# The last channel output in three column pieces, stored from two DMA queues

## The chip, the cores and the metric

One core of one Trainium2 chip (TensorE, VectorE, ScalarE, GpSimd and SyncE, written PE, DVE, ACT, POOL and SP in the profile). The metric is the device time of one execution in microseconds; the kernel before takes 380.88 us (median of 6 runs). A time contains a little under 2 us outside the profile's span: the profiled run of the kernel before took 380.45 us and its span is 378.7 us.

## The reference, cut to what matters

```python
# q, k, v: (8, 12, 448, 64);  x: (8, 448, 768)
scores = scale * (q @ k.transpose(0, 1, 3, 2)) - np.log(S)
x  = merge_heads(sigmoid(scores) @ v)
h  = np.maximum(x.transpose(0, 2, 1) @ w_tok1, 0.0) @ w_tok2   # token mixing
u  = x + h.transpose(0, 2, 1)
h2 = np.maximum(u @ w_ch1, 0.0) @ w_ch2                        # channel mixing
return u + h2                                                  # (8, 448, 768), float32
```

Only the last line matters here: how the last rows of `u + h2` come out of TensorE, through VectorE's addition, to the output in HBM.

## The kernel before: the parts that matter

The kernel is written as operations with dependences and assumed durations. A planner simulates them in Python and so fixes the order in which each engine gets its instructions. The durations are only the planner's assumptions.

A batch has 448 rows, that is 3 blocks of 128 rows and a rest of 64. The rests of two batches share a fourth block: 64 partitions each. So the very last piece of work is `blk == 3` of the last batch: 128 rows (64 of batch 6, 64 of batch 7) by 768 columns.

```python
def channel2(b):
    side = b % 2
    for blk in range(4 if side else 3):
        tiles = (b - 1, b) if blk == 3 else (b,)
        for half in range(2):
            c = slice(DH * half, DH * half + DH)          # DH = 384 columns
            ps = bank(f"c2_{b}_{blk}_{half}", [128, DH])
            def ch2(ps=ps, c=c, blk=blk):
                for cb in range(NCB):                     # NCB = 12
                    w = w_ch2[cb // 4][:, cb % 4, c]
                    if blk < 3:
                        ...                               # one matmul of 128 rows
                    else:
                        for s in range(2):                # two matmuls of 64 rows, side by side
                            nc.tensor.matmul(out=ps[64 * s : 64 * s + 64, :],
                                             lhsT=h2aT[b - 1 + s][:, cb, 384:448], rhs=w, ...)
            ...
            def add(...):                                 # DVE: u = u + psum
                nc.vector.tensor_tensor(out=t, in0=t, in1=ps[:, :], op=ADD)
            a = op(f"y_{b}_{blk}_{half}", "DVE", 0.56, add, ...)
        def store(blk=blk, mine=mine):                    # after both halves are added
            for s in range(2):
                r = slice(64 * s, 64 * s + 64)
                if blk == 3:
                    nc.sync.dma_start(
                        out=out[b - 1 + s].rearrange("(p j) d -> p j d", j=J)[:, 3, :],
                        in_=mine[r, :])
                else:
                    ...                                   # the two row halves go to different rows j
        op(f"st_{b}_{blk}", "SP", 1.3, store, sum_ops[(b, blk)], [mine], rank=2)
```

## Time and profile before

The head of the page of the kernel before: the span, each engine's busy time (with its share of the span and its number of instructions), and the chain of work that ended last, by engine.

```profile
span 378.7 us, 7932 instructions
...
PE 370.8 (98%) x3243; PEld 191.3 (51%) x3243; DVE 160.6 (42%) x296; ACT 205.7 (54%) x252; POOL 118.5 (31%) x265
...
PE 90%; POOL 4%; DMA 2%; ACT 1%; DVE 1%; issue 0%; POOLq 0%
```

TensorE bounds the kernel from start to nearly the end. The change can't touch this. It touches what comes after TensorE's last matmul. The timeline of the kernel before, for this stretch (start in us, duration in us, engine, line, operation, output and inputs, count; in brackets the engine's idle time before and what ended it):

```profile
369.86 4.09 PE L925 MATMUL c<-w_ch,h2aT 128*64 128x384 f16 x48
...
372.11 0.55 DVE L940 TENSOR_TENSOR ut<-ut,c 128x384 f32<-128x384 f32 x1 [1.59 <-PE c L925]
373.99 0.55 DVE L940 TENSOR_TENSOR ut<-ut,c 128x384 f32<-128x384 f32 x1 [1.33 <-PE c L925]
374.57 1.10 SPq L950 DMA_DIRECT2D out_dram<-ut  x2
```

The line of SPq shows only that SP hands two stores to the DMA engines (0.47 and 0.59 us). The Trainium skill ("Perfetto Trace Analysis", section on the HWDGE instruction) warns that the movement of the data lies outside of this window, and here it does: the first packet moves at 375.69 and the last ends at 377.42, while both issues are over by 375.68. So the tail has to be put together from several records. From the start of the last block:

| step in the kernel before | us | cumulated |
|---|---|---|
| first matmul of the last block to the start of its last matmul | 3.77 | 3.77 |
| to the start of the last add | 0.37 | 4.13 |
| last add, 128x384 | 0.55 | 4.69 |
| to the first of the two store issues | 0.03 | 4.72 |
| first issue to the end of the last packet | 2.85 | 7.56 |
| last packet to SP's drain (SP tests that all stores have landed) | 0.44 | 8.00 |
| closing barrier of the engines, to the end of the span | 0.83 | 8.83 |

I shall call the 8.83 us **the tail**: from the first matmul of the last block to the end of the span.

### The profile page before, as it was taken

To read this page: it belongs to the slowest core of one execution; us is meant where nothing else is said; L and a number is where in the kernel's file an instruction comes from. 1 tells how busy PE (TensorE), PEld (TensorE's weight loads), DVE (VectorE), ACT (ScalarE), POOL (GpSimd) and SP (SyncE) were. 2 spreads that over 40 slices of the span, in tenths; PEclk is the share of its full clock that TensorE was granted. 3 is DMA by queue.
4 is the path that set the end of the run, shared out by engine and by line. 5 is a ranking of instruction groups with operands and counts; after the bars stand their busy time and mean duration, and the time that the engine had idled before them with its cause. 6 is when DMAs were issued, how large, how long until landed. Compare 5 with 4: busy or idle time off the path is not lost.

```text
span 378.7 us, 7932 instructions
## 1 busy us (share of the span) xinstructions
PE 370.8 (98%) x3243; PEld 191.3 (51%) x3243; DVE 160.6 (42%) x296; ACT 205.7 (54%) x252; POOL 118.5 (31%) x265
## 2 busy tenths in 40 slices
PE   8999999999999999999999999999999999999994
PEld 4555544555445554445444555444445655555662
DVE  3444434644344323453355313643432365754221
ACT  2987884486757766787678466846664130200000
POOL 9973326344344434444344343430000000000000
PEclk9999999999999999999999999999999999999999
DMA  6999999989987999999999999991103553300353
GB/s 80 181 176 205 208 210 176 153 141 184 146 126 111 174 162 235 146 120 208 190 149 161 162 180 156 145 197 39 30 16 97 113 106 94 73 2 0 85 123 85
DMA packets 98804, 50.56 MB, mean 134 GB/s; under 512 B 72336, under 2 KB 95120, under 8 KB 98768
## 3 DMA queue, kind: packets, MB, share of 16 engines
q0 software_dynamic: 24400, 21.93, 44.2%
q1 hardware_dynamic: 74368, 28.13, 40.8%
q8 instruction: 25, 0.41, 0.4%
q14 instruction: 11, 0.09, 0.1%
HBM read 43.84 MB, written 11.01 MB: 145 GB/s over the span
## 4 chain that ended last, share of the span: by engine, by line
PE 90%; POOL 4%; DMA 2%; ACT 1%; DVE 1%; issue 0%; POOLq 0%
PE c L871 30%; PE c L916 25%; PE qk L542 10%; PE xa L579 8%; PE yn L794 5%; PE k L764 5%; PE c L925 4%; DMA k<-in_k_dram 2%; POOL k L304 1%; POOL q L304 1%; POOL v L304 1%; ACT attn L557 1%; POOL w_tok L337 1%; PE xa L693 1%; PE tk L499 0%
## 5 line engine op out<-in xcount | busy, mean ns | idle before, releaser
L557 ACT ACTIVATE attn<-qk,att_bias 128x896 f16<-128x896 f32 (+1 forms) x172 | 160.9, 987 | 78.6 <-PE qk L542 78.3
L871 PE MATMUL c<-uT,w_ch 128*128 128x448 f16 x576 | 118.0, 353 | 0.1
L916 PE MATMUL c<-w_ch,h2aT 128*128 128x384 f16 x576 | 98.5, 326 | 0.0
L896 DVE TENSOR_SCALAR h2aT<-c 128x448 f16<-128x448 f32 x96 | 59.9, 624 | 77.4 <-PE c L871 77.2
L871 PEld LDWEIGHTS <-w_ch 128*128 128x128 f16 x576 | 53.4, 98 | 56.7 <-issue 11.6
L916 PEld LDWEIGHTS <-h2aT 128*128 128x128 f16 x576 | 55.2, 98 | 40.1 <-issue 4.5
L940 DVE TENSOR_TENSOR u<-u,c 128x384 f32<-128x384 f32 x48 | 26.6, 554 | 77.4 <-PE c L916 77.4
L542 PE MATMUL qk<-qT,kT 64*64 64x448 f16 x672 | 53.1, 363 | 0.2 <-ACT uT L708 0.2
L579 PE MATMUL xa<-attn,v 64*64 64x448 f16 x672 | 36.5, 350 | 0.4 <-ACT attn L557 0.4
L728 POOL COPY mark<-attn 1x1 f16<-1x1 f16 x54 | 9.6, 178 | 80.0 <-ACT attn L557 79.9
L823 ACT ACTIVATE u<-u 128x768 f16<-128x768 f32 x21 | 17.8, 846 | 25.0 <-DVE u L815 25.0
L542 PEld LDWEIGHTS <-kT 64*64 64x64 f16 x672 | 14.5, 104 | 29.8 <-issue 26.9
L815 DVE TENSOR_TENSOR u<-x,yn 128x384 f32<-128x384 f16 x48 | 24.9, 548 | 9.1 <-PE yn L794 9.1
L475 POOL COPY kp<-k 128x384 f16<-128x384 f16 (+1 forms) x54 | 21.2, 427 | 21.0 <-DMA k<-in_k_dram 16.0
L794 PE MATMUL yn<-h,w_tok 128*128 128x384 f16 x128 | 27.4, 328 | 0.0
L579 PEld LDWEIGHTS <-v 64*64 64x64 f16 x672 | 19.6, 107 | 13.2 <-issue 1.6
L612 ACT ACTIVATE xT<-xa 128x448 f16<-128x448 f32 x43 | 21.1, 547 | 9.3 <-PE xa L579 8.1
L475 POOL COPY qp<-q 128x384 f16<-128x384 f16 (+1 forms) x54 | 21.3, 430 | 9.0 <-DMA q<-in_q_dram 8.7
L764 PE MATMUL k<-x,w_tok 128*128 128x384 f16 x112 | 20.6, 327 | 0.1
L776 DVE TENSOR_SCALAR h<-k 128x384 f16<-128x384 f32 x28 | 15.4, 556 | 11.9 <-PE k L764 10.8
L315 POOL DMA_DIRECT2D k<-in_k_dram x21 | 15.0, 716 | 7.4 <-issue 5.9
L794 PEld LDWEIGHTS <-w_tok 128*128 128x128 f16 x128 | 11.0, 98 | 12.1 <-issue 5.9
(57 smaller groups left out, 186.7 us busy)
## 6 DMA issues: line engine op xcount, KB each, us to landing
out_dram<-u SPq DMA_DIRECT2D x48, 192.0 KB, 3.0
k<-in_k_dram POOLq DMA_DIRECT2D x21, 224.0 KB, 5.2
q<-in_q_dram POOLq DMA_DIRECT2D x21, 224.0 KB, 5.5
v<-in_v_dram POOLq DMA_DIRECT2D x21, 224.0 KB, 5.4
w_ch<-in_moe_w_ch_dram POOLq DMA_DIRECT2D x6, 768.0 KB, 15.9
out_dram<-ut SPq DMA_DIRECT2D x8, 192.0 KB, 3.2
v<-in_v_dram POOLq DMA_DIRECT2D x6, 112.0 KB, 4.7
x<-xT SPq DMA_TRANSPOSE x36, 4.6
```

The costliest lines, as they stand in the source:

```text
L475: nc.gpsimd.tensor_copy(out=pm[:, to, :, :], in_=src[:, fr, :, :])
L542: nc.tensor.matmul(out=ps[64 * s : 64 * s + 64, h, 0:S], lhsT=kT[64 * h : 64 * h + 64, i, s, :], rhs=qT[64 * h : 64 * h + 64, :, s, :], st ...
L557: nc.scalar.activation(out=at[:, hs, :], in_=ps[:, hs, 0:S], func=SIGMOID, bias=bias_t[:, :], scale=att_scale,)
L579: nc.tensor.matmul(out=ps[s](slice(64 * h, 64 * h + 64)), lhsT=vf[64 * s : 64 * s + 64, h, order[i], :], rhs=attn[i][64 * s : 64 * s + 64, ...
L612: nc.scalar.activation(out=xt[:, s, c0 : c0 + S], in_=ps[s](every), func=COPYF)
L764: nc.tensor.matmul(out=ps[:, :], lhsT=w_tok1[:, w1_slot(side, blk), 128 * t : 128 * t + 128], rhs=X[b][:, x_block(side, blk), c], start=(b ...
L794: nc.tensor.matmul(out=ps[:, :], lhsT=w_tok2[:, t, s0 : s0 + 2, :], rhs=h1[b][:, t, c], start=(t == 0), stop=(t == 1),)
L815: nc.vector.tensor_tensor(out=to, in0=x, in1=y, op=ADD)
L871: nc.tensor.matmul(out=to(), lhsT=w_ch1[cb // 4][:, db, 128 * (cb % 4) : 128 * (cb % 4) + 128], rhs=uT[b][:, db, :], start=(db == 0), stop ...
L896: nc.vector.tensor_scalar(out=h2aT[b][:, cb, :], in0=to(), scalar1=0.0, scalar2=None, op0=MAX)
L916: nc.tensor.matmul(out=ps[:, :], lhsT=h2aT[b][:, cb, 128 * blk : 128 * blk + 128], rhs=w, start=(cb == 0), stop=(cb == NCB - 1),)
L940: nc.vector.tensor_tensor(out=t, in0=t, in1=ps[:, :], op=ADD)
```

## The change

The intent is to leave less work behind the last matmul. The second half of the last block is cut into two pieces of 192 columns, so that there are three pieces (384, 192, 192). Each is added and stored as soon as it is there, and the two row halves are issued from two queues (SP and the idle ACT) instead of one after the other. Cut to its core:

```diff
-            for half in range(2):
-                c = slice(DH * half, DH * half + DH)
-                ps = bank(f"c2_{b}_{blk}_{half}", [128, DH])
+            final = b == B - 1 and blk == 3
+            cuts = [(0, DH), (DH, 576), (576, D)] if final else [(0, DH), (DH, D)]
+            def store(c=slice(0, D), blk=blk, mine=mine, final=final):
+                for s in range(2):
+                    r = slice(64 * s, 64 * s + 64)
+                    queue = nc.scalar if final and s else nc.sync
+                    if blk == 3:
+                        queue.dma_start(
+                            out=out[b - 1 + s].rearrange("(p j) d -> p j d", j=J)[:, 3, c],
+                            in_=mine[r, c],
+                        )
+                    ...
+            for half, (z0, z1) in enumerate(cuts):
+                c = slice(z0, z1)
+                ps = bank(f"c2_{b}_{blk}_{half}", [128, z1 - z0])
...
-                a = op(f"y_{b}_{blk}_{half}", "DVE", 0.56, add, ...)
+                a = op(f"y_{b}_{blk}_{half}", "DVE", 0.06 + (z1 - z0) * 0.0013, add, ...)
+                if final:
+                    op(f"st_{b}_{blk}_{half}", "SP", 0.7, lambda ...: store(c), [a], [mine], rank=2)
-            op(f"st_{b}_{blk}", "SP", 1.3, store, sum_ops[(b, blk)], [mine], rank=2)
+            if not final:
+                op(f"st_{b}_{blk}", "SP", 1.3, store, sum_ops[(b, blk)], [mine], rank=2)
```

More of the change, by code (lines that the diff above doesn't have):

```diff
@@ L907, in channel2 @@
             tiles = (b - 1, b) if blk == 3 else (b,)
-            for half in range(2):
-                c = slice(DH * half, DH * half + DH)
-                ps = bank(f"c2_{b}_{blk}_{half}", [128, DH])
+            final = b == B - 1 and blk == 3
+            cuts = [(0, DH), (DH, 576), (576, D)] if final else [(0, DH), (DH, D)]
+            mine = ut[b // 2] if blk == 3 else u[b]
+            def store(c=slice(0, D), blk=blk, mine=mine, final=final):
[7 more added lines that the diff above has]
+                        )
+                    else:
+                        j = blk + 4 * (s != side)
+                        queue.dma_start(
+                            out=out[b].rearrange("(p j) d -> p j d", j=J)[:, j, :],
+                            in_=mine[r, blk, :],
+                        )
+            for half, (z0, z1) in enumerate(cuts):
+                c = slice(z0, z1)
+                ps = bank(f"c2_{b}_{blk}_{half}", [128, z1 - z0])
                 def ch2(ps=ps, c=c, blk=blk):
@@ L933, in channel2 @@
                 need = [x for t in tiles for x in ch1_ops[t]] + ch2_ld
-                o = op(f"C2_{b}_{blk}_{half}", "PE", 12 * mm(DH), ch2, need, [ps, *(h2aT[t] for t in tiles), *w_ch2])
+                o = op(f"C2_{b}_{blk}_{half}", "PE", 12 * mm(z1 - z0), ch2, need, [ps, *(h2aT[t] for t in tiles), *w_ch2])
                 ops.append(o)
-                mine = ut[b // 2] if blk == 3 else u[b]
                 def add(ps=ps, c=c, blk=blk, mine=mine):
@@ L942, in channel2 @@
                 sums = [x for t in tiles for x in u_ops[t]]
-                a = op(f"y_{b}_{blk}_{half}", "DVE", 0.56, add, [o, *sums], [ps, mine], rank=-1)
+                a = op(f"y_{b}_{blk}_{half}", "DVE", 0.06 + (z1 - z0) * 0.0013, add, [o, *sums], [ps, mine], rank=-1)
                 sum_ops.setdefault((b, blk), []).append(a)
-            def store(blk=blk, mine=mine):
-                for s in range(2):
-                    r = slice(64 * s, 64 * s + 64)
-                    if blk == 3:
-                        nc.sync.dma_start(
-                            out=out[b - 1 + s].rearrange("(p j) d -> p j d", j=J)[:, 3, :],
-                            in_=mine[r, :],
-                        )
-                    else:
-                        j = blk + 4 * (s != side)
-                        nc.sync.dma_start(
-                            out=out[b].rearrange("(p j) d -> p j d", j=J)[:, j, :],
-                            in_=mine[r, blk, :],
-                        )
-            op(f"st_{b}_{blk}", "SP", 1.3, store, sum_ops[(b, blk)], [mine], rank=2)
+                if final:
+                    op(f"st_{b}_{blk}_{half}", "SP", 0.7, lambda store=store, c=c: store(c), [a], [mine], rank=2)
+            if not final:
+                op(f"st_{b}_{blk}", "SP", 1.3, store, sum_ops[(b, blk)], [mine], rank=2)
         return ops
```

## The prediction

> **What bounds the kernel.** TensorE: the page gives PE 370.8 us busy (98%) of a 378.7 us span, and the chain that ended last is 90% PE. The change touches only the end. In the timeline the last block (48 matmuls, 64 output rows by 384 columns) starts at 369.86, its last matmul at 373.62. What follows is a tail of 5.1 us without TensorE:
>
> - last add, 128x384: 373.99 to 374.54 (0.55 us);
> - two store issues on the SP queue, one after the other: 374.57 (0.47 us), 375.09 (0.59 us);
> - packets from 375.69 to 377.41 (8 of 3072 bytes on each engine, 121 to 250 ns each);
> - SP sees the last landing at 377.79; then 0.9 us of closing barrier, to 378.69.
>
> **What changes.** The second half of the last block becomes two pieces of 192 columns; each of three pieces is added and stored alone (six issues instead of two), half of the rows from SP, half from ACT, idle since about 330 us. The bytes (384 KB) stay.
>
> 1. TensorE: a pair of matmuls starts every 162 ns at 384 columns; I estimate 82 at 192. Weight loads should not bind: the transposes, also 64-column pairs, start every 55 ns. 24 pairs of 82 instead of 12 of 162: +0.03 us.
> 2. Last add: VectorE groups 256, 384, 448 columns wide (424, 556, 624 ns) give 1.04 ns a column, so 0.35 us at 192: -0.20.
> 3. Issue: the last row half no longer queues behind the other: up to -0.5. The Trainium skill ("DMA: Bandwidth & Descriptors", section on issuing engines) says that several issuing engines save only the sequencer's issue time; "Perfetto Trace Analysis" (HWDGE instruction) has the descriptor generator locked by one at a time. No run shows yet whether the lock eats this; I count half, -0.25.
> 4. Data: after the last issue 96 KB are left (8 packets of 768 bytes an engine) instead of 384 KB; the rest goes out while TensorE and VectorE still work. 1.7 us of packets become about 0.6 to 0.9 (packets of 896 bytes, another queue, took 87 ns): -0.8, the largest term.
> 5. Receipt (0.38 us from last packet to SP) and barrier (0.9 us) stay.
>
> All of it is on the critical path: nothing else runs there. Sum: about -1.2 us; less a little for a slow first issue on ACT (5 of 56 store issues on SP took 1.4 to 1.6 us): -1.1 us.
>
> **Predicted: 379.8 us, 8 in 10 between 379.0 and 380.6. Faster by over 2%: 0.01; within 2%: 0.97; slower by over 2%: 0.02.** The trace's span should be about 377.6 instead of 378.7.
>
> **What would show each step.** Pairs of 192 columns 80 to 90 ns apart (over 110: weight-bound) (1); last add about 354 ns (2); SP's and ACT's last issues starting within 50 ns of each other, ACT's lasting near 0.5 (no lock) or near 1.0 us (lock) (3); last packet 0.7 to 1.1 us after the last piece's first, before 376.7 (4); last landing seen at 376.4 to 377.0, 0.9 us from there to the end (5).
>
> **What would make it wrong.** (a) ACT's first issues are slow and pile up. (b) The adds wait for the earlier piece's store to finish reading the shared tile: +1 to +3 us. (c) The kernel's planner gets a marginally different duration for every channel add (0.5592 instead of 0.56) and may order earlier work differently: a microsecond either way. (d) Small rows land no faster, as fixed latency governs: gain only 0.3 to 0.5 us.

## The result

| | median us | lowest to highest | runs |
|---|---|---|---|
| before | 380.88 | 380.54 to 380.92 | 6 |
| changed | 380.44 | 379.62 to 381.07 | 6 |

The ratio of the times is 0.9991, with a 95% interval of 0.9978 to 1.0003. (A ratio is the mean time of one kernel's runs over that of the other's of the same rounds, so not quite the ratio of the medians above.) So this first look shows a gain of about 0.4 us that can't be told from none. In the profile the span went from 378.7 to 378.6 us. Yet the tail is clearly shorter. The timeline of the changed kernel:

```profile
370.65 4.12 PE L945 MATMUL c<-w_ch,h2aT 128*64 128x384 f16 x72
...
372.90 0.55 DVE L959 TENSOR_TENSOR ut<-ut,c 128x384 f32<-128x384 f32 x1 [1.59 <-PE c L945]
373.48 2.18 SPq L917 DMA_DIRECT2D out_dram<-ut  x3
373.49 2.21 ACTq L917 DMA_DIRECT2D out_dram<-ut  x3
373.82 0.35 DVE L959 TENSOR_TENSOR ut<-ut,c 128x192 f32<-128x192 f32 x1 [0.37 <-PE c L945]
374.81 0.35 DVE L959 TENSOR_TENSOR ut<-ut,c 128x192 f32<-128x192 f32 x1 [0.64 <-PE c L945]
```

The first line counts all 72 matmuls of the last block under its first shape; 48 of them have 192 columns. Two things are to be seen. First, the last block begins at 370.65 instead of 369.86: the changed kernel reached its changed part 0.79 us later. Second, from there on it is faster: its tail is 7.91 us instead of 8.83.

| step | before | changed | difference |
|---|---|---|---|
| first to last matmul of the last block (starts) | 3.77 | 3.88 | +0.11 |
| to the start of the last add | 0.37 | 0.29 | -0.08 |
| last add | 0.55 | 0.36 | -0.20 |
| to the last piece's first issue | 0.03 | 0.03 | 0.00 |
| that issue to the end of the last packet | 2.85 | 1.78 | -1.07 |
| last packet to SP's drain | 0.44 | 0.74 | +0.30 |
| closing barrier | 0.83 | 0.85 | +0.02 |
| tail | 8.83 | 7.91 | -0.92 |

The view of the DMA issues for the end of both kernels (output and input, queue, operation, count, KB of each, median us from issue to landing). Before:

```profile
out_dram<-ut SPq DMA_DIRECT2D x2, 192.0 KB, 2.7
```

Changed:

```profile
out_dram<-ut SPq DMA_DIRECT2D x1, 96.0 KB, 2.1
out_dram<-ut ACTq DMA_DIRECT2D x1, 96.0 KB, 2.4
out_dram<-ut SPq DMA_DIRECT2D x2, 48.0 KB, 1.9
out_dram<-ut ACTq DMA_DIRECT2D x2, 48.0 KB, 2.1
```

A store of 48 KB needs 1.9 us on SP's queue against 2.7 for 192 KB: a quarter of the bytes takes about 70% of the time.

Three questions are left: why the block started later, where the +0.30 at the end comes from, and which half of the change (the pieces or the second queue) does the work.

### The profile page after: what moved, and what is told of

Same layout as the page of the kernel before. It is cut to its first block, busy times and chain, and to the rows that moved or that the text cites. A ratio compares the mean times of both kernels' runs of the same rounds, so it can differ in the third digit from the quotient of the medians.

```text
span 378.6 us, 7990 instructions
## 1 busy us (share of the span) xinstructions
PE 370.4 (98%) x3267; PEld 191.6 (51%) x3267; DVE 161.0 (43%) x297; ACT 205.9 (54%) x252; POOL 118.4 (31%) x265
## 4 chain that ended last, share of the span: by engine, by line
PE 90%; DMA 3%; POOL 3%; ACT 1%; DVE 1%; issue 0%; POOLq 0%
PE c L871 30%; PE c L936 25%; PE qk L542 10%; PE xa L579 8%; PE yn L794 5%; PE k L764 5%; PE c L945 4%; DMA k<-in_k_dram 3%; ACT attn L557 1%; POOL k L304 1%; POOL q L304 1%; POOL w_tok L337 1%; PE xa L693 1%; PE tk L499 0%; PE xb L632 0%
```

## The experiments

Twelve kernels ran. All gave a correct result. All of them list the same instructions in the same order on every engine up to the last block, apart from the stores named below; this was compared in the built programs, and the records of PE's matmuls, DVE and ACT in the 14 traces agree with it. "Tail" is always read from the kernel's own trace. Times of whole runs scatter by a microsecond.

### The same two kernels again

No edit. Theory A: the later start of the last block is chance. Rival B: the change slows the start of the kernel.

> The kernel before, unchanged, as a control. Theory A (the change gains about 0.9 us in the tail, and the rest of the difference between the two traces is chance in the loading phase): the tail, from the start of the last block's first matmul to the end of the span, is again 8.8 us (8.83 in the first trace), the time from one build of it to another scatters by some tenths, ratio 1.000 within 0.002; the moment at which the last block starts may differ from 369.86 by up to 0.8 us. Rival B (the change slows the start of the kernel): the last block starts within 0.2 us of 369.86 again.

> The changed kernel, unchanged, as a second look. Theory A: the tail from the last block's first matmul is again 7.9 us, while the start of the last block moves from its 370.65, and the time lies about 0.9 us under the kernel before (ratio 0.9976). Rival B: the last block starts again near 370.6, and the ratio is again near 0.999.

| trace | last block starts | tail | time, median us (range) | ratio to before |
|---|---|---|---|---|
| before, first | 369.86 | 8.83 | 380.88 (380.54 to 380.92) | |
| before, again | 371.32 | 8.82 | 381.40 (380.94 to 383.50) | 1.0011 (0.9984 to 1.0038) |
| changed, first | 370.65 | 7.91 | 380.44 (379.62 to 381.07) | 0.9991 (0.9978 to 1.0003) |
| changed, again | 370.05 | 7.90 | 379.95 (379.54 to 382.03) | 0.9975 (0.9946 to 1.0004) |

The tails repeat to 0.01 us; the start of the last block moved by 1.46 us between two executions of an identical kernel, and this time the changed kernel's came earlier. So theory A holds: the 0.79 us were chance. Here is where it arises. Per stretch of time: us, then busy time (and instructions) of PE, PEld, DVE, ACT and POOL, granted clock, DMA share, GB/s. Before, first trace:

```profile
10.00:25.00 15.00, 14.19 (x188) 7.60 (x184) 6.52 (x15) 14.05 (x19) 14.57 (x22) 1.00 1.19 177
25.00:41.00 16.00, 15.02 (x217) 8.55 (x218) 9.08 (x18) 13.20 (x19) 5.91 (x11) 1.00 1.25 203
41.00:369.00 328.00, 327.83 (x2739) 167.58 (x2735) 139.91 (x251) 175.23 (x212) 88.77 (x213) 1.00 0.84 131
```

The same kernel again:

```profile
10.00:25.00 15.00, 13.68 (x186) 7.47 (x186) 6.24 (x14) 13.09 (x18) 13.29 (x21) 1.00 1.14 167
25.00:41.00 16.00, 14.82 (x192) 8.05 (x192) 8.70 (x17) 13.45 (x19) 6.42 (x10) 1.00 1.24 202
41.00:369.00 328.00, 327.67 (x2751) 167.56 (x2752) 140.14 (x251) 176.34 (x213) 89.47 (x215) 1.00 0.83 131
```

While the first inputs are being loaded, the DMA brought 177 GB/s in one execution and 167 in the other, and PE worked less. The lag changes mostly at PE's transposes of q and k, which need the inputs that are being loaded; the largest single step (from 0.4 to 1.2 us) is at this group, which waited in the second execution and not in the first. First trace, then the second:

```profile
17.34 0.58 PE L499 MATMUL tk<-ident,k 128*64 128x128 f16 x14
18.58 0.58 PE L499 MATMUL tk<-ident,k 128*64 128x128 f16 x14 [0.84 <-DMA k<-in_k_dram]
```

After about 41 us PE is busy without a gap and both executions run in parallel: the second lags by 1.45 us at 41 us and by 1.46 us at the last block. Here, what the loading phase gave is carried to the end unchanged; in two of the 14 traces a further 0.3 and 0.5 us came later (at 70 us in the kernel with the two stores swapped, at 140 us in that with the pieces on one queue; both come below). Over all 14 traces the last block starts anywhere from 369.86 to 371.32 us.

### Which half of the change does the work: pieces on one queue, and two queues without pieces

```diff
-                    queue = nc.scalar if final and s else nc.sync       # changed kernel
+                    queue = nc.sync
```

> The changed kernel with all six stores on SP's queue; ACT issues none. Theory A for the queues: the second queue saves only part of an issue, since in the changed kernel ACT's last packets began 0.27 us after SP's although both issues began together; so the tail is 0.2 to 0.3 us longer than with two queues, 8.1 to 8.2 us. If each issue really ran alone on its queue, the loss would be a whole issue, 0.5 us. Rival B in the form that the use of ACT's queue slows the start: the last block starts near 369.9 instead of 370.6, and the time is lower than the changed kernel's.

```diff
                     if blk == 3:                                         # kernel before
-                        nc.sync.dma_start(
+                        queue = nc.scalar if b == B - 1 and s else nc.sync
+                        queue.dma_start(
```

> The kernel before with only the second of the last two stores moved to ACT's queue; no pieces. Theory A: the two stores are bound by their 384 KB of packets (1.7 us), so the second queue gains almost nothing: tail 8.6 to 8.9 us instead of 8.83. If the issue were what counts, it would be 8.3. Rival B (use of ACT's queue slows the start): last block starts near 370.6 and the ratio is 1.001 to 1.002.

| | one queue | two queues |
|---|---|---|
| whole (one store for each row half) | 8.83 | 8.86 |
| three pieces | 9.02 | 7.91 |

The table gives the tails in us. In whole times the pieces on one queue had a median of 381.03 us and a ratio of 0.9994 (0.9970 to 1.0017), the two queues without pieces 381.54 us and 1.0003 (0.9981 to 1.0025).

Neither part is worth anything alone. Two queues without pieces gave nothing (+0.03), as expected. Pieces on one queue lost 0.2 us, and my expectation (8.1 to 8.2, or 8.4) was far off. The timeline of the pieces on one queue shows why:

```profile
373.08 0.55 DVE L959 TENSOR_TENSOR ut<-ut,c 128x384 f32<-128x384 f32 x1 [1.59 <-PE c L945]
373.66 3.67 SPq L917 DMA_DIRECT2D out_dram<-ut  x6
...
374.99 0.35 DVE L959 TENSOR_TENSOR ut<-ut,c 128x192 f32<-128x192 f32 x1 [0.64 <-PE c L945]
```

SP issues six stores from 373.66 to 377.33 almost without a pause, about 0.6 us each. The last add is done at 375.35, but SP is still busy with the stores of the middle piece; the last piece's stores go out at 376.15 and 376.74. A queue that spends 1.2 us on a piece can't keep up with pieces that come 0.72 and 0.99 us apart. I had counted the second queue as half of one issue (0.25 us) by looking only at the last pair of stores. It is worth 1.11 us with three pieces and nothing with one.

The Trainium skill ("DMA: Bandwidth & Descriptors", section on issuing engines) says that several issuing engines only save the sequencer's issue time, which is usually small beside the DMA itself. The first part agrees with these runs. The second, which the page limits by "usually", doesn't hold for these small stores: the packets of a 48 KB store took 0.37 us, its issue on SP 0.47 to 0.59 (from issue to landing it is 1.9 us). That the queues do share something shows in the changed kernel: SP's and ACT's last issues started within 4 ns of each other, but ACT's first packet moved 0.27 us after SP's (376.58 and 376.31).

### The order of SP's last tests

A semaphore is a counter; in the trace, that of a store reaches its full count when the store has landed (S118 of the kernel before at 377.776; SP's test of it passes at 377.793). At the end SP tests one semaphore after another, eight of them (S111 to S118) for the DMAs of SP and ACT, always in the same order. Each such DMA takes the next of the eight in turn. From the trace records of SP (start in us, semaphore number), the last three tests and the drain before, and the last seven in the changed kernel:

```
before    376.102 S116   377.209 S117   377.793 S118   377.858 drain
changed   376.452 S112   377.341 S113   377.403 S114   377.462 S115   377.524 S116   377.583 S117   377.645 S118   377.710 drain
```

Before, the last two stores have S117 and S118: when S118 is there, SP is done. With four more stores, the last two have S113 and S114. SP waits for S113 until 377.341 and must then still test five others that were satisfied long ago, 62 ns each. The test: shift the last stores to S117 and S118 by four more issues, well before the end (the cut stores are issued 7 to 14 us before the last pair in the trace, not 15 as the expectation has it).

```diff
                     else:                                                # changed kernel
-                        queue.dma_start(out=...[:, j, :], in_=mine[r, blk, :])
+                        for z in [slice(0, DH), slice(DH, D)] if b == B - 1 and blk < 2 else [slice(0, D)]:
+                            queue.dma_start(out=...[:, j, z], in_=mine[r, blk, z])
```

> The changed kernel, but four more store issues about 15 us earlier (two earlier stores cut in half by columns), so that the last two stores get the last two of the eight semaphores that SP tests one after another before the end. Theory: in the changed kernel SP's last real wait is followed by five tests of long landed stores, 62 ns each, 0.31 us; here none or one is left, so the time from the last packet to SP's drain falls from 0.74 to about 0.44 us and the tail from the last block's start from 7.90 to 7.60 us. Rival: the tests after the last landing are not what fills this time (the landing itself is late); then the tail stays at 7.9.

The time from the last packet to the drain fell from 0.74 to 0.50 us and the tail from 7.91 to 7.66 (expected 7.60; one test of 62 ns is left, since ACT's store, the later one, got S117 and not S118: SP passes S117 at 376.650, S118 at 376.712, and the drain is at 376.777). Median 379.94 us, ratio 0.9971 (0.9946 to 0.9997). The theory holds: the +0.30 us of the result are SP's tests of stores that had already landed.

### What the size of the last piece is worth

```diff
-            cuts = [(0, DH), (DH, 576), (576, D)] if final else [(0, DH), (DH, D)]
+            cuts = [(0, DH), (DH, D)] if final else [(0, DH), (DH, D)]
```

> The changed kernel with two pieces of 384 columns instead of 384, 192, 192; each stored alone on the two queues. Theory (after the last add, 192 KB instead of 96 KB wait for packets, and the last add is 0.55 instead of 0.355 us): tail 8.3 us, half way between 8.82 before and 7.90 after. Rival (what counts is the two queues and fixed latency, not the size of the last piece): tail 8.0 to 8.1, only the add's 0.2 us longer.

Tail 8.42 us; median 380.01 us, ratio 0.9971 (0.9948 to 0.9993). This is on the side of the theory (8.3), not of the rival (8.0 to 8.1). Against the changed kernel the last piece's packets end 0.25 us later after their issue, the last add is 0.20 us longer, and SP has two more tests to go through (0.12 us); TensorE saves 0.03. So the cut of the second half is worth 0.5 us of the 0.92; 0.12 of this is the place of the semaphores and not the size of the piece, and without it the tail would be the 8.3 of the theory.

### One store of 128 rows instead of two of 64

The rows of the two batches lie at one constant distance in the output (64 partitions times 7 rows are just the 448 rows of a batch), so that both row halves of the last block can be stored by one DMA. First with nothing else changed in the kernel before:

```diff
+                if b == B - 1 and blk == 3:
+                    nc.sync.dma_start(
+                        out=out[b - 1 : b + 1].rearrange("s (p j) d -> (s p) j d", j=J)[:, 3, :],
+                        in_=mine[:, :])
+                    return
```

> The kernel before with its last two stores joined to one DMA of 128 rows; no pieces, no second queue. Theory (bound by 384 KB of packets from 1.1 us after the issue): tail 8.6 to 8.9, as with two queues. If the second issue had cost its 0.5 us: 8.3.

The timeline of this kernel:

```profile
374.21 0.55 DVE L940 TENSOR_TENSOR ut<-ut,c 128x384 f32<-128x384 f32 x1 [1.33 <-PE c L925]
374.79 0.36 SPq L948 DMA_DIRECT2D out_dram<-ut  x1
```

The tail is 8.01 us, far under the expected 8.6 to 8.9: this one edit gains 0.82 us, nearly as much as the whole change. Median 380.14 us, ratio 0.9976 (0.9953 to 0.9998). I had held the 1.7 us of packets for a property of 384 KB. It was one of two stores of 64 rows. The stretches of time around the packets (columns as above; only the last two numbers matter, DMA share and GB/s), before:

```profile
375.50:376.50 1.00, 0.00 (x0) 0.00 (x0) 0.00 (x0) 0.00 (x0) 0.00 (x0) 1.00 0.87 181
376.50:377.50 1.00, 0.00 (x0) 0.00 (x0) 0.00 (x0) 0.00 (x0) 0.00 (x0) 0.99 0.69 212
```

With one store of 128 rows:

```profile
375.50:376.50 1.00, 0.00 (x0) 0.00 (x0) 0.00 (x0) 0.00 (x0) 0.00 (x0) 1.00 0.86 338
376.50:377.50 1.00, 0.00 (x0) 0.00 (x0) 0.00 (x0) 0.00 (x0) 0.00 (x0) 1.00 0.15 55
```

The engines are as busy (0.87 and 0.86) but move nearly twice as much. From the packet records: both kernels send 128 packets of 3072 bytes. They take 193 ns each on average and 1.73 us together before, 124 ns each and 1.13 us in one store. In addition the issue is shorter (0.36 us instead of 0.47 for half of the rows), and the first packet moves 0.85 us after the issue began instead of 1.12.

The Trainium skill says to use 128 rows: "DMA: Bandwidth & Descriptors" (Rules for kernel authors) calls two transfers to the two halves of the partitions useless, as they serialize, and recommends one of 128; "SBUF — State Buffer" (Door 1) explains that 64 partitions reach only half of the 16 ports. The advice is borne out (384 KB in 1.73 us against 1.13 us, that is 228 against 347 GB/s). The explanation fits only in part: in the kernel before the 64 packets that start first take 233 ns on average, but the other 64 take 152, most of them 121, and they come from only half of the partitions, too. Is it that rows 0 to 63 are slow? The last experiment swapped the two stores:

```diff
-                for s in range(2):
+                for s in (1, 0) if b == B - 1 and blk == 3 else (0, 1):
```

> The kernel before with its last two stores in the other order: rows 64 to 127 first, rows 0 to 63 second; nothing else. In the kernel before the 64 packets that start first (rows 0 to 63) take 233 ns on average and the other 64 take 152, with most of these at 121; one store of 128 rows has 124 for all. Theory P (rows 0 to 63 alone are slow to read): now the first store has packets near 125 and the second near 235. Theory F (whichever store of 64 rows comes first is slow): again about 233 first and 152 after. Under either the tail stays within 0.2 us of 8.82, and the time within the scatter of the kernel before.

The first 64 packets, now of rows 64 to 127, took 235 ns and the others 151; the tail was 8.83 us; median 380.86 us, ratio 0.9997 (0.9983 to 1.0012). So it is whichever store comes first, not a row range. That the slow packets belong to the first store is an inference from their order where both stores share a queue. In the kernel with two queues and no pieces the queue tells them apart. Its two issues:

```profile
374.87 0.47 SPq L951 DMA_DIRECT2D out_dram<-ut  x1
374.87 0.55 ACTq L951 DMA_DIRECT2D out_dram<-ut  x1
```

Both start within 5 ns, yet ACT's packets begin at 377.01, 1.03 us after SP's first (375.99) and 0.20 us before SP's last ends (377.21); SP's take 255 ns on average and ACT's 124. So the two stores ran nearly one after the other on two queues as well, which fits that the second queue alone gained nothing.

Is a store of 64 rows slow by itself, then, or only as the first of two? A trace says the former. The kernel that cuts four earlier stores in two (from the section on SP's tests) has seven stores of 64 rows and half the width, 1536 bytes a packet, whose packets end before those of the next store begin. They take 106 to 109 ns on average, in both row halves; packets of 1536 bytes in a store of 128 rows (three joined pieces, below) take 67. So the slow packets are those that a store of 64 rows has when it runs alone, which agrees with that explanation. Why the second of two that follow each other directly is faster stays open.

### Joined stores in pieces: versions with a shorter tail than both kernels

```diff
-            cuts = [(0, DH), (DH, 576), (576, D)] if final else [(0, DH), (DH, D)]      # changed kernel
+            cuts = [(0, 512), (512, D)] if final else [(0, DH), (DH, D)]
...
+                if final:
+                    nc.sync.dma_start(
+                        out=out[b - 1 : b + 1].rearrange("s (p j) d -> (s p) j d", j=J)[:, 3, c],
+                        in_=mine[:, c])
+                    return
                 for s in range(2):
```

> Two pieces of 512 and 256 columns; each is stored by one DMA of 128 rows on SP's queue, ACT's is unused. Theory: what the second queue gives is that no issue waits behind another (six in a row on SP cost 1.1 us); two issues that carry all rows do the same on one queue, if an issue of 128 rows takes about as long as one of 64 (0.47 us), and the last semaphores are again the last that SP tests. Tail 7.6 us, and the time 1.2 us under the kernel before (0.9968). If an issue of 128 rows takes twice as long: 8.1.

Tail 7.20 us, 0.71 under the changed kernel, on a single queue and with only two issues. It beat the expectation (7.6) because the expectation still assumed what a store of 64 rows needs; the issue took 0.33 us and its packets ended 1.35 us after it began, instead of 1.78 in the changed kernel. Median 379.13 us, ratio 0.9950 (0.9929 to 0.9972). Its timeline:

```profile
373.00 0.69 DVE L965 TENSOR_TENSOR ut<-ut,c 128x512 f32<-128x512 f32 x1 [2.23 <-PE c L951]
373.71 1.30 SPq L914 DMA_DIRECT2D out_dram<-ut  x2
374.24 0.42 DVE L965 TENSOR_TENSOR ut<-ut,c 128x256 f32<-128x256 f32 x1 [0.55 <-PE c L951]
```

Then three pieces (384, 256, 128), once as they are and once with seven more issues before (stores of the last batch's first two blocks, cut by columns), so that the last store again gets the last semaphore:

```diff
+            cuts = [(0, DH), (DH, 640), (640, D)] if final else [(0, DH), (DH, D)]
...
+                        n = {(0, 0): 3, (0, 1): 3, (1, 0): 3, (1, 1): 2}.get((blk, s), 1) if b == B - 1 else 1
+                        for i in range(n):                # only in three_joined_late
+                            z = slice(D // n * i, D // n * (i + 1))
```

> Three pieces of 384, 256 and 128 columns, each stored by one DMA of 128 rows on SP's queue. Against two pieces of 512 and 256 (tail 7.20 us from the last block's start), the last add is 0.13 us and the last packets about 0.25 us shorter, so the landing is seen 0.3 us earlier; but there are three stores, so the last one gets the first of the eight semaphores that SP tests at the end, and seven tests of 62 ns (0.43 us) follow the last landing. Theory: tail 7.3 us. Rival (the order of SP's tests costs nothing): 6.9.

> The same, with seven more store issues some 10 to 20 us earlier (stores of the blocks before are cut by columns), so that the last store gets the last of the eight semaphores. Theory: tail 6.9 us, 0.4 less than without, and the best of all; time 1.9 us under the kernel before (0.995). If the extra issues hold up SP's queue, more.

> The two pieces of 512 and 256 columns with joined stores once more, beside the three pieces on the same chip: tail again 7.20 us; time about 1.6 us under the kernel before (0.9957), against 0.995 in the first call.

| kernel | tail | last packet to drain | median us (range) | ratio to before |
|---|---|---|---|---|
| three pieces, joined | 7.38 | 0.86 | 379.45 (379.08 to 380.08) | 0.9961 (0.9948 to 0.9974) |
| the same, last semaphore | 6.95 | 0.43 | 379.00 (378.74 to 379.83) | 0.9954 (0.9941 to 0.9966) |
| two pieces, joined, again | 7.19 | 0.43 | 379.93 (378.92 to 381.42) | 0.9980 (0.9962 to 0.9998) |

Here both expectations of the tail were met (7.3 and 6.9). Seven tests of 62 ns are 0.43 us, and that is just what the shift of the semaphore saves: without it a third piece is worse than none, with it better. The end of the best kernel's timeline:

```profile
373.04 1.98 SPq L914 DMA_DIRECT2D out_dram<-ut  x3
373.70 0.42 DVE L968 TENSOR_TENSOR ut<-ut,c 128x256 f32<-128x256 f32 x1 [0.69 <-PE c L954]
374.37 0.29 DVE L968 TENSOR_TENSOR ut<-ut,c 128x128 f32<-128x128 f32 x1 [0.25 <-PE c L954]
```

Its tail is 1.88 us under that of the kernel before, twice the gain of the change. The two looks at the two joined pieces (ratios 0.9950 and 0.9980, tails 7.20 and 7.19) show once more how little whole times can tell here: the loading phase adds up to 1.5 us of scatter, the tail 0.01.

## Why the prediction was right or wrong

The forecast was 379.8 us, with a range of 379.0 to 380.6; the result 380.44 us lies in the range. This is in part luck: another six runs of the same kernel had 379.95, and the medians of the kernel before went from 380.85 to 381.40 between one set of runs and another. The forecast gain was 1.1 us. In the medians it was 0.44 us, in the second look 1.3 us (379.95 against 381.29 for the kernel before), and in the tail, which is the only thing that the change touches, 0.92 us in two pairs of traces. Point by point:

- **TensorE, +0.03 us: right.** Pairs of 192 columns start 82.5 ns apart, and from the first matmul to the start of the last add it is +0.03 us (4.13 to 4.16). The weight loads don't bind.
- **Last add, -0.20 us: right.** 355 ns, forecast about 354.
- **Issue and data, -0.25 and -0.8 us: the sum right, partly by luck, and the picture incomplete.** From the last piece's issue to the last packet it is -1.07 us, and all of it is packets: from the first to the last it is 0.66 us instead of 1.73, while the first packet still comes 1.12 us after the issue. The 1.73 us were also not what 384 KB need, as step 4 took them, but what two stores of 64 rows need: one store of 128 rows takes 1.13. The second queue took nothing off the last pair of issues by itself (tail 8.86 without pieces). Both last issues start within 4 ns, and ACT's took 0.50 us, so no lock shows in that duration (the middle piece's took 0.68 against SP's 0.47, started together), but its packets came 0.27 us after SP's. What the second queue is really for (to keep six issues from piling up, 1.11 us) the prediction didn't see.
- **Receipt and barrier stay: wrong, and this is the step that was mis-sized.** The receipt itself stayed: SP saw the last landing 0.37 us after the last packet, as before. But the term from the last packet to SP's drain grew from 0.44 to 0.74 us, because the last stores no longer held the last of the semaphores that SP tests in turn. In the terms of the prediction, the 0.9 us from the landing seen to the end became 1.21. This took back 0.30 of the 1.2 us. Moving the last stores to the last semaphores gave 0.25 us back.
- **Risks.** (a) ACT's issues took 0.56, 0.68 and 0.50 us: no pile-up. (b) The adds didn't wait for an earlier piece's store: before the last add DVE was released by PE (its line above). (c) The planner's new durations left the order of all earlier instructions as it was. (d) Small rows did land with less gain than their size promised, but more than 0.3 to 0.5 us.
- **What the prediction lacked altogether** is the scatter of the loading phase: up to 1.46 us between two executions of one kernel, more than the effect that was to be forecast. The three runs known beforehand agreed within 0.4 us and hid it. A narrower range would have been luck.

## What to carry to other kernels

For work behind the last matmul, count from the last add to the last receipt and see what each store holds up: cut the last output so that most of it has left before the last piece is ready, but only as fine as the issuing queue can keep up with, and store all 128 rows with one DMA wherever the addresses allow it. That single join gained 0.82 us here, almost as much as pieces and a second queue together, and with two pieces it beat them on one queue. When the effect is smaller than the scatter of whole runs, measure it in the trace from a fixed point just before the change.

## What the Trainium skill lacked or had wrong

- No page that I read tells that SP's tests at the end of a kernel cost time after the last landing: 62 ns each, in a fixed order, 0.31 us in the changed kernel and 0.43 us in the three joined pieces. Which semaphore the last store gets decides it.
- "DMA: Bandwidth & Descriptors" calls the issue time usually small relative to the DMA. For stores of 48 KB the issue (0.47 to 0.59 us) was longer than the packets (0.37 us), though not than the 1.9 us from issue to landing, and issuing three pieces from one queue instead of two cost 1.11 us.
- The same page doesn't say that a store of 128 rows is also issued faster: 0.33 to 0.36 us against 0.47 us for 64 rows, with the first packet 0.82 to 0.85 us after the start of the issue instead of 1.12.
- "SBUF — State Buffer" (Door 1) explains the slowness of 64 partitions by half of the ports. Stores of 64 rows that ran alone agree (106 to 109 ns a packet of 1536 bytes against 67 with 128 rows). But of two that follow each other directly the first had packets of 233 ns and the second of 152 ns, in either order of the rows, against 124 ns for 128 rows. The ports alone don't explain the difference between the two.
- "TensorE: Matmul & The Clock Gate" (LDWEIGHTS) gives a weight load as its number of columns over 1.2 per ns, from which I estimate 53 ns for 64 columns and 107 ns for two loads one after the other. Here pairs of 64-column loads came every 82.5 ns with 192-column matmuls and every 55 ns with the transposes. In the last block the two loads of a pair start 3 to 4 ns apart (their records last 106 to 111 ns): the loads for the two column halves overlap, which that section doesn't say.
- No page that I read warns that the loading phase of one and the same kernel scatters: 167 and 177 GB/s between 10 and 25 us in two executions of the same kernel, and 1.46 us in the start of the last block.
